# Queries and keys of pairs 1 to 7 laid out by transfers from a transposed input, in a fused attention and mixture kernel

## The chip, the cores and the metric

The kernel runs on one core of one Trainium2 chip. The metric is the device time of one execution in microseconds (us). TensorE is called PE below, its weight loads PEld; VectorE is DVE, ScalarE is ACT, GpSimd is POOL, and SP is the engine whose queue issues nearly all transfers.

## The reference, cut to what matters

Three stages follow each other. The change touches the first one alone, an attention in which a query sees only keys of its own cluster:

```
q_n, k_n, c_n = rows of q, k, centroids divided by (norm + 1e-6)
q_assign = argmax(q_n . c_n), k_assign = argmax(k_n . c_n)      # 16 clusters
mask   = q_assign == k_assign
scores = where(mask, 0.125 * q @ k.T, -1e9)
attn   = softmax(scores)
out    = attn @ v                                               # 2 batches, 8 heads, 768 x 64
```

The output, as 1536 tokens of 512 features, goes through a dense layer pair of width 2048 with softplus (`moe_w_in`, `moe_w_out`), and then through eight experts of width 1024 whose weights are mixed by a balanced gate (`moe2_*`). `moe_w_in` and `moe_w_out` arrive as float64 and are turned into float32 on the chip.

## The kernel before

Every product is taken with operands that are split in two: a rounded part (hi, type fp32r) and the remainder (lo), so that sums of products keep float32 accuracy.

The attention handles the 16 heads as 8 pairs `g` = 0 to 7, each of two heads `j` = 0, 1 of one batch. `w` = 0 stands for the query, `w` = 1 for the key. Per pair there is a preparation and then the attention itself.

The preparation of a pair: `pair_load` (L312) brings q, k and v as `raw` tiles, with the tokens on the partitions. `pair_split` (L326) makes hi and lo of q (scaled by 0.125) and k, side by side in `QS` and `KS`: for pair 0 on ACT and DVE, for the others on POOL (L344 to L346). `pair_trans` (L384) transposes them on PE, three blocks of 128 tokens into one PSUM tile `pt` (L393), eight such groups per pair; ACT copies each group to the tile `AT[w, j]` (L395), in which 64 rows hold hi and 64 rows lo; and a transfer copies the hi rows into `Bt[w, j]` (L397). `pair_norm` takes the squares of the raw tiles on ACT (L356), halves them three times on POOL and sums on DVE, and makes the norms. `pair_sims` (L401) multiplies the stacked `AT` by the normalised centroids in `Z` (L413), `pair_simsT` turns the result back, `pair_argmax` finds the cluster of each token, and `pair_ohT` transposes the one-hot codes into `OHT` and sends them by four transfers into rows 64 to 79 of the four `Bt` tiles (L476).

The attention of a pair has four halves of 384 queries each (head `j`, half `hf`), and each half six steps: `score` multiplies `AT` and then `Bt` (L532), where `Bt` adds the missing product of the two hi parts and the mask; DVE takes the maximum (L540), ACT the exponential (L545); `e_trans` transposes the result on PE (L572), ACT makes its hi part (L575) and DVE its lo part (L579); `av` multiplies by v (L587); `merge` finishes.

All groups that PE transposes or makes in the preparation, `pt` among them, and the transposed exponentials `t` share one PSUM pool of three tiles (`ps_t`, tag "t").

The order of the work is written as events with a step number; a pair takes `SP` = 24 steps, pair `g` begins its attention at step 24g, its scores 8 steps before. `sched_pair(g, b0)` places the preparation around `b0` = 24g - 34. The events are traced in the order of their steps, and a scheduler that works before the run then fixes the order of instructions on every engine, where it may bring an instruction forward. For the categories in `KEEP`, each instruction stays behind the last one traced so far on its engine.

`fetch_first` loads the float64 weights of the first unit of the dense layers (call 0, four transfers of 512 KB, L135 and L139) and converts them (calls 1 to 4) while the attention still runs; call 0 is placed at step 84 and is not in `KEEP`.

Of the kernel before, what the change touches and what calls it, by code (L numbers as in the profile page):

```python
# [7 lines left out]
F32 = mybir.dt.float32  # L8
# [11 lines left out]
@with_exitstack  # L20
def attention_moe_moe2(ctx, tc, q, k, v, centroids, w_in, w_out, w_gate, w1, w2, eye, out, dbg=None):
    nc = tc.nc
# [229 lines left out]

    Z = pp.tile([P, H, 224], F32R, tag="Z", name="Z", bufs=1)

# [7 lines left out]
    def prep_centroids():  # L262
        nc.vector.memset(Z.bitcast(F32), 0.0)
        craw = pp.tile([P, D], F32, tag="craw", name="craw", bufs=1)
# [18 lines left out]
    def prep_z(c2):  # L283
        for i in range(2):
            pc = ps_m.tile([P, P], F32R, tag="t", name=f"pc{i}")
            nc.tensor.transpose(pc, c2[:, i].rearrange("p a d -> p (a d)"), idr)
            nc.vector.tensor_copy(
                Z[:, :, 96 + 16 * i : 112 + 16 * i],
                pc.bitcast(F32).rearrange("p (h c) -> p h c", h=H),
            )  # L290

    def last_of_engines():
        found = {}
        for ins in reversed(nc.cur_bb.bb.instructions[-400:]):
            en = str(ins.engine).split(".")[-1]
            if en in ("PE", "DVE", "Activation", "Pool"):
                found.setdefault(en, ins)
        return found.values()  # L300
# [11 lines left out]
    def pair_load(g):  # L312
        b, hp = divmod(g, NPAIR)
        st = pairs[g] = Pair()
        st.b, st.hp, st.g = b, hp, g
        st.raw = []
# [7 lines left out]
        st.AT, st.Bt = {}, {}  # L324

    def pair_split(st, n):  # L326
        g = st.g
        rq, rk, rv = st.raw
        if n == 0:
            st.QS = pp.tile([P, 2, NT, 2 * D], F32R, tag="QS", name=f"QS{g}", bufs=1)  # L330
            st.KS = pp.tile([P, 2, NT, 2 * D], F32R, tag="KS", name=f"KS{g}", bufs=1)
        j, w = divmod(n, 2)
# [3 lines left out]
        else:  # L336
            hi, lo = st.KS[:, j, :, D:], st.KS[:, j, :, 0:D]
        if g == 0:
            sc = 0.125 if w == 0 else 1.0
            nc.scalar.activation(hi, r, AF.Copy, scale=sc)  # L340
            nc.vector.scalar_tensor_tensor(lo, r, sc, hi.bitcast(F32), ALU.mult, ALU.subtract)
            return
        if w == 0:
            nc.gpsimd.tensor_scalar(r, r, 0.125, 0.0, ALU.mult, ALU.add)  # L344
        copy_r(hi, r)
        nc.gpsimd.tensor_tensor(lo, r, hi.bitcast(F32), ALU.subtract)  # L346

    def pair_norm(st, n):
# [5 lines left out]
        if n < 2:  # L354
            r = st.raw[n]
            nc.scalar.activation(r, r, AF.Square, scale=8.0 if n == 0 and g else 1.0)  # L356
        elif n < 4:
# [43 lines left out]
    def pair_sims(st, hf, ph):  # L401
        g = st.g
        if ph == 0:
# [3 lines left out]
            st.sm = ps_m.tile([P, CB], F32, tag="t", name=f"sm{g}{hf}")  # L407
            n = 0
            for w in range(2):
                for j in range(2):  # L410
                    h = 2 * st.hp + j
                    o = 64 * w + 32 * j
                    nc.tensor.matmul(  # L413
                        st.sm, Z[:, h, 96 - o : 224 - o], st.AT[w, j][:, hf * CB : (hf + 1) * CB],
                        start=n == 0, stop=n == 3,
                    )
                    n += 1
        else:
# [61 lines left out]
    def sched_pair(g, b0):  # L480
# [8 lines left out]
        at(b0 - 12.13, lambda: pair_load(g))  # L489
        for n in range(4):  # L490
            P_(b0 - 7.54 + 1.5 * n, "sp", pair_split, n)
        for n in range(2):
            P_(b0 + n + 1.54, "sq", pair_norm, n)
# [3 lines left out]
        P_(b0 + (12.5 if g else 8.37), "nv", pair_norm, 6)  # L497
        for i in range(8):
            d = 1.09 * i
# [519 lines left out]
```

## Time and profile before

| | |
|---|---|
| median of 3 runs | 1630.16 us (1629.44 to 1633.29) |
| the profiled execution | 1626.59 us |
| its span, first to last instruction | 1624.8 us |
| mean granted PE clock | 0.995 |
| busy share of the span | PE 96%, PEld 86%, DVE 67%, ACT 53%, POOL 43% |
| last result of the attention begins (L603) | 300.9 us |

The span begins at the first instruction, so that all times of the trace are counted from there. Some 300 us of it are attention, the rest the two dense stages. Busy times are unions of the instructions' spans on one engine; since matmuls overlap in the pipeline, the time that a group of them costs is read from one group's start to the next one's start, not from the duration of one.

### The profile page before, as it was taken

The page shows a single profiled execution, that of the slowest core. Times are in us where ns is not written, and L with a number is a line of the kernel's source. Part 1 is how long each engine was busy: PE and PEld are TensorE (multiplying, and loading weights), DVE is VectorE, ACT ScalarE, POOL GpSimd, SP SyncE. Part 2 cuts the span into 40 slices and gives each one's busy share as a digit, 9 for nine tenths or more (in the row PEclk, how much of TensorE's full clock was granted, in tenths as well). Part 3 has the DMA queues.
Part 4 walks back from the last instruction along what each step waited for, and adds up shares of the span by engine and source line. Part 5 has one row for each costly group of instructions (what it writes and reads, how often), then busy time and mean ns, then how long its engine had stood idle before and what let it go on. Part 6 is the DMA issues. An engine that isn't in the chain of part 4 may idle for free.

```text
span 1624.8 us, 22972 instructions
## 1 busy us (share of the span) xinstructions
PE 1554.7 (96%) x8302; PEld 1392.2 (86%) x8302; DVE 1085.4 (67%) x1768; ACT 861.6 (53%) x1769; POOL 705.5 (43%) x729
## 2 busy tenths in 40 slices
PE   5999999889899989999999999999999999999999
PEld 5878888888797868899999999988999999999997
DVE  6998889998744677745556566577556556565553
ACT  6888888766666664434344344345434344343442
POOL 6544543233656652433344344345343443433330
PEclk9999999999999999999999999999999999999999
DMA  6233220256112121223222322314222232222311
GB/s 195 61 93 91 67 52 6 84 196 200 60 53 78 52 66 40 78 73 81 69 78 69 81 74 67 88 53 125 58 84 71 70 88 62 78 76 74 78 53 46
DMA packets 129474, 128.67 MB, mean 79 GB/s; under 512 B 8048, under 2 KB 99664, under 8 KB 129360
## 3 DMA queue, kind: packets, MB, share of 16 engines
q1 hardware_dynamic: 129216, 127.14, 27.7%
q8 instruction: 65, 1.06, 0.3%
q14 instruction: 49, 0.40, 0.1%
q10 hardware_dynamic: 144, 0.07, 0.0%
HBM read 107.72 MB, written 11.58 MB: 73 GB/s over the span
## 4 chain that ended last, share of the span: by engine, by line
PE 64%; DVE 6%; ACT 4%; issue 1%; POOL 1%; DMA 0%; DVEq 0%; SPq 0%; POOLq 0%; ACTq 0%
PE Y L813 32%; PE la L685 16%; PE mb L685 8%; PE lb L685 4%; PE y L794 2%; DVE gf L761 1%; DVE gl L775 1%; DVE wl L226 1%; ACT u L759 1%; ACT gh L774 1%; ACT u L758 1%; PE p L738 1%; ACT wh L225 1%; ACT u L760 0%; DVE xS L75 0%
## 5 line engine op out<-in xcount | busy, mean ns | idle before, releaser
L774 ACT CAST gh<-gf 128x384 fp32r<-128x384 f32 x316 | 161.3, 512 | 482.9 <-DVE gf L768 438.1
L214 POOL TENSOR_TENSOR wf<-wf 128x256 f32<-128x256 f32 x288 | 239.3, 852 | 351.7 <-DMA wf<-in_moe_w_dram 302.1
L232 POOL TENSOR_TENSOR w2l<-w2f,w2h 128x512 fp32r<-128x512 f32 x160 | 241.3, 1528 | 307.9 <-ACT w2h L231 307.9
L813 PE MATMUL Y<-w2h,gh 128*128 128x512 f32 x768 | 299.0, 389 | 0.6 <-ACT gh L774 0.6
L813 PE MATMUL Y<-w2l,gh 128*128 128x512 f32 x768 | 298.9, 389 | 0.0
L813 PE MATMUL Y<-w2h,gl 128*128 128x512 f32 x768 | 298.5, 389 | 0.0
L775 DVE TENSOR_TENSOR gl<-gf,gh 128x384 fp32r<-128x384 f32 x316 | 208.2, 662 | 96.0 <-ACT gh L774 89.3
L712 DVE TENSOR_TENSOR gf<-la,c 128x384 f32<-128x384 f32 x71 | 39.5, 557 | 253.3 <-PE la L685 253.2
L225 ACT CAST wh<-wf 128x512 fp32r<-128x512 f32 (+1 forms) x232 | 153.0, 684 | 35.1 <-PE la L685 24.3
L813 PEld LDWEIGHTS Y<-w2h,gl 128*128 128x128 f32 x768 | 144.2, 188 | 30.0
L813 PEld LDWEIGHTS Y<-w2h,gh 128*128 128x128 f32 x768 | 144.0, 187 | 22.2 <-ACT gh L774 1.1
L813 PEld LDWEIGHTS Y<-w2l,gh 128*128 128x128 f32 x768 | 144.2, 188 | 21.1
L768 DVE SCALAR_TENSOR_TENSOR gf<-gf,pb 128x384 f32<-128x384 f32 x177 | 153.6, 869 | 4.0
L226 DVE TENSOR_TENSOR wl<-wf,wh 128x512 fp32r<-128x512 f32 (+1 forms) x194 | 152.3, 811 | 1.5 <-ACT wh L225 1.5
L579 DVE TENSOR_TENSOR el<-t,eh 128x384 fp32r<-128x384 f32 x192 | 103.1, 547 | 18.9 <-ACT eh L575 17.4
L572 PE MATMUL t<-idf,E 128*128 128x128 f32 x576 | 97.9, 280 | 11.0 <-ACT OHT L471 3.7
L575 ACT CAST eh<-t 128x384 fp32r<-128x384 f32 x192 | 92.5, 484 | 24.1 <-PE t L572 12.5
L685 PE MATMUL mb<-chS,wh 128*128 128x384 f32 x288 | 98.2, 341 | 4.3 <-DVE gf L708 3.9
L231 ACT CAST w2h<-w2f 128x512 fp32r<-128x512 f32 x160 | 92.2, 617 | 16.8 <-PE y L794 8.6
L685 PE MATMUL la<-chA,wh 128*128 128x384 f32 x288 | 98.0, 340 | 1.7 <-DVE gf L768 1.7
L685 PE MATMUL la<-chS,wh 128*128 128x384 f32 x288 | 97.8, 340 | 0.3 <-ACT c L704 0.2
L540 DVE TENSOR_REDUCE sc<-s 128x1 f32<-128x768 f32 x96 | 90.8, 947 | 10.5 <-PE s L532 10.2
(210 smaller groups left out, 3524.6 us busy)
## 6 DMA issues: line engine op xcount, KB each, us to landing
w2f<-in_moe_w_dram SPq DMA_DIRECT2D x128, 256.0 KB, 3.3
wf<-in_moe_w_dram SPq DMA_DIRECT2D x128, 256.0 KB, 3.4
r<-in_moe_w_in_dram SPq DMA_DIRECT2D x16, 512.0 KB, 5.3
r<-in_moe_w_out_dram SPq DMA_DIRECT2D x16, 512.0 KB, 5.2
Bt<-AT SPq DMA_DIRECT2D x32, 192.0 KB, 2.7
pb<-pdram SPq DMA_DIRECT2D x15, 384.0 KB, 8.0
w<-wf SPq DMA_DIRECT2D x16, 256.0 KB, 3.7
w<-w2f SPq DMA_DIRECT2D x16, 256.0 KB, 3.4
```

Of the source, the lines that this page charges most:

```text
L214: nc.gpsimd.tensor_tensor(wf[:, SLOT[o_], :], wf[:, SLOT[u_], :], wf[:, SLOT[v_], :], ALU.subtract)
L225: nc.scalar.copy(wh[:, c0:c1], wf[:, c0 + o : c1 + o, :])
L226: (nc.vector if kind == 2 or u == (1, 0, 0, 0) else nc.gpsimd).tensor_tensor(wl[:, c0:c1], wf[:, c0 + o : c1 + o, :], wh[:, c0:c1].bitcast ...
L232: nc.gpsimd.tensor_tensor(w2l[:, c], w2f[c], w2h[:, c].bitcast(F32), ALU.subtract)
L572: nc.tensor.transpose(pt[:, t * P : (t + 1) * P], Et[i, t][:, s * P : (s + 1) * P], idf)
L575: nc.scalar.copy(eh, TT[i, s])
L579: nc.vector.tensor_tensor(el, TT.pop((i, s)), EHL[i, s].bitcast(F32), ALU.subtract)
L685: nc.tensor.matmul(ps, wt[:, s_, ks], xx[:, k_, :], start=i in (0, 1, 3) and n == 0, stop=n == 3 * nk - 1, skip_group_check=True,)
L768: nc.vector.scalar_tensor_tensor(g, src, 0.0, PB[sb, e][:, cols], ALU.max, ALU.mult)
L774: nc.scalar.copy(gh[:, cols], g)
L775: nc.vector.tensor_tensor(gl[:, cols], g, gh[:, cols].bitcast(F32), ALU.subtract)
L813: nc.tensor.matmul(y[m], gt[:, ms], wt[:, q, :], start=first and i == 0, stop=last and i == 2)
```

## The change

For pairs 1 to 7 the queries and keys are also given to the kernel transposed (`qt`, `kt`: 64 features by 768 tokens for each head, with the tokens in the order of the kernel's partition layout). The arrays are laid out on the host, ahead of the launch.

- `pair_load` brings two more tiles `rT` (128 partitions: two heads by 64 features; 768 tokens; 384 KB each) ahead of q, k and v.
- A new `pair_split_t` splits them in three phases: ACT writes hi of both heads at once (128x768, scaled for q); POOL scales the q tile and subtracts, 128x768 each; then for each head three transfers of 64 rows (192 KB each) put hi and lo into `AT` and hi into `Bt`: 12 transfers per pair in place of the four of L397. The third phase (`sp2`) is in `KEEP`, behind the last SP instruction alone.
- `pair_split` and `pair_trans` remain for pair 0. The raw q tile is no longer scaled in place, so the squares are taken with scale 1.
- `pair_sims` multiplies, for these pairs, the split tile `HL` of both heads by a `Z` that has one block per head: four matmuls per half as before. Pair 0 keeps the old form with a tile `Z0` of its own. `prep_centroids` clears `Z0` (128x448) on DVE and `Z` (128x768) on POOL, where DVE cleared 128x1792; `prep_z` fills both with six copies on DVE in place of two.
- `HL` takes the places of `QS` and `KS` (one buffer for each of q and k).
- `b0` is 24g - 38 for pairs 2 to 7, four steps earlier; pairs 0 and 1 keep theirs.
- `fetch_first(0)` moves from step 84 to step 14 and goes into `KEEP` (category `fr`, SP alone): its four loads come behind the last SP instruction traced by then.

```
+        if g:
+            for w, src in enumerate((qt, kt)):
+                t = pp.tile([P, S], F32, tag=f"rT{w}", name=f"rT{w}{g}", bufs=1)
+                nc.sync.dma_start(t, src[b, 2 * hp : 2 * hp + 2].rearrange("j d s -> (j d) s"))
+                st.rT.append(t)
...
+    def pair_split_t(st, w, ph):
+        g = st.g
+        r, sc = st.rT[w], 1.0 if w else 0.125
+        if ph == 0:
+            st.HL[w] = pp.tile([P, 2, S], F32R, tag=f"HL{w}", name=f"HL{w}{g}", bufs=1)
+            nc.scalar.activation(st.HL[w][:, 0], r, AF.Copy, scale=sc)
+            return
+        hi, lo = st.HL[w][:, 0], st.HL[w][:, 1]
+        if ph == 1:
+            if w == 0:
+                nc.gpsimd.tensor_scalar(r, r, sc, 0.0, ALU.mult, ALU.add)
+            nc.gpsimd.tensor_tensor(lo, r, hi.bitcast(F32), ALU.subtract)
+            return
+        for j in range(2):
+            js = slice(j * D, (j + 1) * D)
+            t = st.AT[w, j] = ap.tile([P, S], F32R, tag=f"AT{g % 2}{w}{j}", name=f"AT{g}{w}{j}", bufs=1)
+            u = st.Bt[w, j] = ap.tile([80, S], F32R, tag=f"Bt{g % 2}{w}{j}", name=f"Bt{g}{w}{j}", bufs=1)
+            for dst, src in ((t[w * D : (w + 1) * D], hi), (t[(1 - w) * D : (2 - w) * D], lo), (u[0:D], hi)):
+                nc.sync.dma_start(dst.bitcast(F32), src[js].bitcast(F32))
...
+                if g:
+                    c, m = Z[:, st.hp, 64 - 64 * w : 192 - 64 * w], st.HL[w][:, x]
+                else:
+                    o = 64 * w + 32 * x
+                    c, m = Z0[:, x, 96 - o : 224 - o], st.AT[w, x]
+                nc.tensor.matmul(st.sm, c, m[:, hf * CB : (hf + 1) * CB], start=n == 0, stop=n == 3)
...
-        for n in range(4):
+        for n in range(4) if g == 0 else ():
             P_(b0 - 7.54 + 1.5 * n, "sp", pair_split, n)
+        for w in range(2) if g else ():
+            for ph in range(2):
+                P_(b0 - 7 + 0.5 * ph + 3 * w, f"sp{ph}", pair_split_t, w, ph)
+            P_(g * SP - 31 + 2 * w, "sp2", pair_split_t, w, 2)
...
-        for i in range(8):
+        for i in range(8) if g == 0 else ():
             d = 1.09 * i
             P_(b0 + d + 0.5, "t0", pair_trans, i, 0)
...
-        sched_pair(g, g * SP - LEAD - 26)
+        sched_pair(g, g * SP - LEAD - (30 if g > 1 else 26))
...
-    at(92 - 8, lambda: fetch_first(0))
+    at(14, lambda: fetch_first(0), ("fr", 0))
...
-                for ins in last_of_engines():
+                for ins in last_of_engines(("SP",) if cat[0] in ("fr", "sp2") else ("PE", "DVE", "Activation", "Pool")):
```

## Rows read from the trace of the kernel before

**Rows 1.** The page: busy time of each engine over the whole span.
```profile
PE 1554.7 (96%) x8302; PEld 1392.2 (86%) x8302; DVE 1085.4 (67%) x1768; ACT 861.6 (53%) x1769; POOL 705.5 (43%) x729
```

**Rows 2.** Windows between the one-hot transfers: start:end, length, busy (instructions), clock, DMA share, GB/s.
```profile
core 0: us, PE busy (x) PEld busy (x) DVE busy (x) ACT busy (x) POOL busy (x), PEclk, DMA share, GB/s
50.83:89.40 38.57, 35.07 (x235) 31.14 (x233) 36.44 (x69) 33.81 (x78) 19.08 (x28) 1.00 0.24 64
89.40:124.84 35.44, 33.18 (x218) 28.46 (x218) 34.05 (x66) 31.19 (x73) 18.80 (x28) 1.00 0.38 107
124.84:159.14 34.30, 32.59 (x218) 28.46 (x218) 30.32 (x60) 29.80 (x71) 17.61 (x28) 1.00 0.37 102
193.27:227.40 34.13, 32.45 (x218) 28.51 (x218) 29.36 (x58) 29.69 (x71) 17.63 (x28) 1.00 0.21 53
261.54:295.67 34.13, 32.34 (x210) 29.15 (x210) 30.91 (x57) 28.30 (x63) 12.09 (x12) 1.00 0.04 7
```

**Rows 3.** Groups by line on PE, 193.27 to 227.40: count, busy us, mean ns.
```profile
L413 PE MATMUL sm<-AT,Z 128*128 128x384 f32 x8 | 1.8, 346 | 0.0
L393 PE MATMUL pt<-idr,KS 128*128 128x128 f32 x12 | 1.6, 245 | 0.0
L393 PE MATMUL pt<-idr,QS 128*128 128x128 f32 x12 | 1.6, 241 | 0.0
...
L427 PE MATMUL tp<-idf,sT 128*128 128x128 f32 x6 | 1.0, 272 | 0.0
L465 PE MATMUL po<-idr,OH 128*64 128x128 f32 x6 | 0.7, 224 | 0.0
```

**Rows 4.** Timeline of PE in that window: start, length, instruction, idle before.
```profile
198.77 0.45 PE L393 MATMUL pt<-idr,KS 128*128 128x128 f32 x3
199.29 0.55 PE L572 MATMUL t<-idf,E 128*128 128x128 f32 x3
...
200.67 0.38 PE L393 MATMUL pt<-idr,QS 128*128 128x128 f32 x3
200.88 0.52 PE L572 MATMUL t<-idf,E 128*128 128x128 f32 x3
...
204.23 0.34 PE L587 MATMUL av<-el,VV 128*128 128x384 f32 x1
204.89 0.55 PE L572 MATMUL t<-idf,E 128*128 128x128 f32 x3 [0.32 <-ACT AT L395]
```

**Rows 5.** Windows: the transposing part of that pair, then the rest of it.
```profile
193.27:206.60 13.33, 12.81 (x90) 11.22 (x90) 10.88 (x22) 13.11 (x33) 7.64 (x13) 1.00 0.47 116
206.60:227.40 20.80, 19.64 (x130) 17.29 (x129) 18.47 (x37) 16.57 (x40) 9.99 (x16) 1.00 0.05 12
```

**Rows 6.** Groups by line on ACT and POOL, 193.27 to 227.40.
```profile
L395 ACT CAST AT<-pt 128x384 fp32r<-128x384 f32 x8 | 3.8, 486 | 0.0
...
L356 ACT ACTIVATE rawq<-rawq 128x768 f32<-128x768 f32 x1 | 0.9, 862 | 0.0
...
L346 POOL TENSOR_TENSOR QS<-rawq,QS 128x384 fp32r<-128x384 f32 x2 | 2.0, 1017 | 0.0
...
L49 POOL TENSOR_SCALAR KS<-rawk 128x384 fp32r<-128x384 f32 x2 | 1.0, 514 | 0.1
```

**Rows 7.** Windows that hold one `Bt<-AT` copy, and two raw loads with one copy.
```profile
231.40:234.40 3.00, 2.93 (x19) 2.32 (x19) 2.46 (x4) 3.00 (x8) 2.77 (x5) 1.00 0.29 66
...
201.50:206.00 4.50, 4.18 (x32) 3.67 (x31) 3.95 (x8) 4.28 (x13) 2.81 (x6) 1.00 0.80 202
```

**Rows 8.** Timeline of SP's queue, one pair: start, time to issue, transfer.
```profile
193.27 2.44 SPq L476 DMA_DIRECT2D Bt<-OHT  x4
197.26 3.60 SPq L397 DMA_DIRECT2D Bt<-AT  x2
201.50 0.37 SPq L319 DMA_DIRECT2D rawq<-in_q_dram  x1
203.39 0.46 SPq L397 DMA_DIRECT2D Bt<-AT  x1
```

**Rows 9.** Start of the kernel: two windows with the granted clock, then the timeline.
```profile
20.00:24.00 4.00, 1.90 (x13) 1.41 (x13) 2.32 (x4) 1.66 (x4) 3.88 (x4) 0.54 0.55 147
24.00:28.00 4.00, 4.00 (x24) 3.83 (x23) 0.26 (x1) 2.80 (x7) 2.34 (x4) 0.61 0.46 95
...
9.51 0.47 DVE L287 CAST Z<-pc 128x128 fp32r<-128x128 f32 x2
...
22.57 0.50 PE L465 MATMUL po<-idr,OH 128*64 128x128 f32 x3 [0.48 <-DVE OH L458]
23.09 0.84 ACT L395 CAST AT<-pt 128x384 fp32r<-128x384 f32 x2
...
23.82 0.85 ACT L471 CAST OHT<-po 64x384 fp32r<-64x384 f32 x2
```

More of the change, by code (lines that the diff above doesn't have):

```diff
@@ L20, in attention_moe_moe2 @@
 @with_exitstack
-def attention_moe_moe2(ctx, tc, q, k, v, centroids, w_in, w_out, w_gate, w1, w2, eye, out, dbg=None):
+def attention_moe_moe2(ctx, tc, q, k, v, qt, kt, centroids, w_in, w_out, w_gate, w1, w2, eye, out, dbg=None):
     nc = tc.nc
@@ L251, in attention_moe_moe2 @@
         nc.gpsimd.memset(wsel[:, :, c : c + 1], float(NC_ - c))
-    Z = pp.tile([P, H, 224], F32R, tag="Z", name="Z", bufs=1)
+    Z = pp.tile([P, NPAIR, 192], F32R, tag="Z", name="Z", bufs=1)
+    Z0 = pp.tile([P, 2, 224], F32R, tag="Z0", name="Z0", bufs=1)
     def norm_newton(o, x, s0, eng):
@@ L262, in prep_centroids @@
     def prep_centroids():
-        nc.vector.memset(Z.bitcast(F32), 0.0)
+        nc.vector.memset(Z0.bitcast(F32), 0.0)
+        nc.gpsimd.memset(Z.bitcast(F32), 0.0)
         craw = pp.tile([P, D], F32, tag="craw", name="craw", bufs=1)
@@ L286, in prep_z, with last_of_engines @@
             nc.tensor.transpose(pc, c2[:, i].rearrange("p a d -> p (a d)"), idr)
[L287 to L294, printed above, removed]
+            pv = pc.bitcast(F32).rearrange("p (h j c) -> p h j c", j=2, c=NC_)
+            nc.vector.tensor_copy(Z0[:, :, 96 + 16 * i : 112 + 16 * i], pv[:, 0])
+            for j in range(2):
+                js, o = slice(j * D, (j + 1) * D), 64 + 32 * j + 16 * i
+                nc.vector.tensor_copy(Z[js, :, o : o + NC_], pv[js, :, j])
+    def last_of_engines(engines):
         found = {}
@@ L297, in last_of_engines @@
             en = str(ins.engine).split(".")[-1]
-            if en in ("PE", "DVE", "Activation", "Pool"):
+            if en in engines:
                 found.setdefault(en, ins)
@@ L315, in pair_load @@
         st.b, st.hp, st.g = b, hp, g
+        st.AT, st.Bt, st.rT, st.HL = {}, {}, [], {}
+        if g:
[3 more added lines that the diff above has]
+                st.rT.append(t)
         st.raw = []
@@ L323, in pair_load @@
             st.raw.append(t)
-        st.AT, st.Bt = {}, {}
     def pair_split(st, n):
@@ L329, in pair_split @@
         if n == 0:
-            st.QS = pp.tile([P, 2, NT, 2 * D], F32R, tag="QS", name=f"QS{g}", bufs=1)
-            st.KS = pp.tile([P, 2, NT, 2 * D], F32R, tag="KS", name=f"KS{g}", bufs=1)
+            st.QS, st.KS = (
+                pp.tile([P, 2, NT, 2 * D], F32R, tag=f"HL{w}", name=f"QK{w}", bufs=1) for w in range(2)
+            )
         j, w = divmod(n, 2)
@@ L337, in pair_split @@
             hi, lo = st.KS[:, j, :, D:], st.KS[:, j, :, 0:D]
[L338 to L341, printed above, removed]
-            return
[L343 to L346, printed above, removed]
+        sc = 0.125 if w == 0 else 1.0
+        nc.scalar.activation(hi, r, AF.Copy, scale=sc)
+        nc.vector.scalar_tensor_tensor(lo, r, sc, hi.bitcast(F32), ALU.mult, ALU.subtract)
+    def pair_split_t(st, w, ph):
[4 more added lines that the diff above has]
+            nc.scalar.activation(st.HL[w][:, 0], r, AF.Copy, scale=sc)
+            return
+        hi, lo = st.HL[w][:, 0], st.HL[w][:, 1]
[4 more added lines that the diff above has]
+            return
+        for j in range(2):
+            js = slice(j * D, (j + 1) * D)
[3 more added lines that the diff above has]
+                nc.sync.dma_start(dst.bitcast(F32), src[js].bitcast(F32))
     def pair_norm(st, n):
@@ L355, in pair_norm @@
             r = st.raw[n]
-            nc.scalar.activation(r, r, AF.Square, scale=8.0 if n == 0 and g else 1.0)
+            nc.scalar.activation(r, r, AF.Square, scale=1.0)
         elif n < 4:
@@ L407, in pair_sims @@
             st.sm = ps_m.tile([P, CB], F32, tag="t", name=f"sm{g}{hf}")
[L408 to L417, printed above, removed]
+            for n in range(4):
+                w, x = divmod(n, 2)
+                if g:
[4 more added lines that the diff above has]
+                nc.tensor.matmul(st.sm, c, m[:, hf * CB : (hf + 1) * CB], start=n == 0, stop=n == 3)
         else:
@@ L635, in attention_moe_moe2 @@
         at(175 + n * 5, lambda n=n: x_split("1_0", first_blk, n), ("xs", 0))
-    KEEP = {'sq': 1, 'red': 1, 'av': 1, 'am3': 1, 'tpa': 1, 'smc': 0, 'm0': 1, 'nw': 0, 'nv': 1, 'rw': 1, 'pz': 1, 'e1': 1, 'ln': 0}
+    KEEP = {'sp2': 1, 'fr': 0, 'sq': 1, 'red': 1, 'av': 1, 'am3': 1, 'tpa': 1, 'smc': 0, 'm0': 1, 'nw': 0, 'nv': 1, 'rw': 1, 'pz': 1, 'e1': 1, 'ln': 0}
     events.sort(key=lambda x: x[:2])
@@ L988, in attention_moe_moe2 @@
         run(steps.get(9, []))
-_INS = ["q", "k", "v", "centroids", "moe_w_in", "moe_w_out", "moe2_w_gate", "moe2_w1", "moe2_w2", "eye"]
+_INS = ["q", "k", "v", "qt", "kt", "centroids", "moe_w_in", "moe_w_out", "moe2_w_gate", "moe2_w1", "moe2_w2", "eye"]
 _OUTS = [((1536, 512), "float32")]
@@ L1004 @@
     inputs["eye"] = _np.eye(128, dtype=_np.float32)
+    for name in "qk":
+        a = _np.asarray(inputs[name])
+        b, h, n, d = a.shape
+        inputs[name + "t"] = a.reshape(b, h, 128, n // 128, d).transpose(0, 1, 4, 3, 2).reshape(b, h, d, n)
     for name in _INS:
```

## Prediction

> **What bounds the kernel now.** I read the page first: PE is busy for 96% of the span [rows 1], so a change pays when it takes time off PE's path. An average says nothing about one stage, so I cut the attention into windows that begin and end with the one-hot transfers of successive pairs [rows 2]. From 124.84 us on a pair takes 34.1 to 34.3 us, the same from pair to pair, and in each PE is busy for 32.5 us (95%), DVE for 29.4 to 30.3 (86 to 88%), ACT for 29.7 (87%). The two windows before that are longer, 38.57 and 35.44 us, and there DVE is the fullest engine, 36.44 and 34.05 us (94 and 96%): the weight conversions lie there. The window from 261.54 holds no preparation of a later pair, and shows what preparation costs: 210 matmuls in 34.13 us, where a pair with preparation has 218, of which 24 `pt`, 8 `sm`, 6 `tp` and 6 `po` [rows 2, 3] are preparation. The other 174 would take 34.13 x 174 / 210 = 28.3 us. Preparation thus costs 5.8 us per pair on the path that sets the end.
>
> Which part of the pair holds that cost? The part in which the eight `pt` groups are transposed, 13.33 us long, has PE busy for 12.81 and ACT for 13.11 us (98%) [rows 5]. In the rest ACT has 4.2 us free. So in the very stretch from which the change takes work, PE and ACT are both full, and DVE has 2.4 us to spare.
>
> **The change part by part, pairs 1 to 7.**
>
> PE loses the 24 `pt` matmuls. Their summed busy time is 3.2 us per pair [rows 3], but they overlap; from the start of one group of three to the next instruction it is 0.21 us [rows 4], so eight groups cost 1.7 us. Around them PE also waits for PSUM tiles that the copy of L395 has yet to free: 0.3 us of the 0.52 between the starts at 198.77 and 199.29, and 0.3 to 0.5 of the 0.66 between those at 204.23 and 204.89 [rows 4]. PE's gain per pair is therefore 1.7 us at least, 2.5 with these waits, and 3.2 if the full busy time counted. `sm` stays at eight matmuls of 384 columns, with other operands of the same shape: nothing.
>
> ACT loses eight copies of 486 ns, 3.8 us, and gains two of 128x768. No row shows this form; the square of the same shape takes 862 ns [rows 6], so 1.7 us. ACT gains 2.1 us per pair, and in the full stretch all 3.8, since hi is now placed at steps 3 and 6 of a pair, away from it.
>
> POOL loses 2 x 0.52 (L344, as L49), 4 x 0.51 and 4 x 1.02 us [rows 6], 7.2 in all, and gains one scaling and two subtractions of twice the size, 1.0 + 2 x 2.0 = 5.0 us. POOL is half idle [rows 2]; this gives nothing to the time.
>
> DVE has no term per pair. That is the limit of the gain: with 29.4 us of work at the 96% that it reached in the window of 89.40, a pair can't come under 30.6 us, a gain of 3.5.
>
> Transfers: one copy of 192 KB takes 0.29 of 3.00 us, 0.87 us of all 16 DMA engines, and a raw load (0.80 x 4.50 - 0.87) / 2 = 1.37 us [rows 7]. Eight more copies and two more loads are 9.7 us per pair, beside a share of 0.21 [rows 2] that is 7.2 us: 16.9 of about 31.5, so there is room on average. They are hidden by the lead: `sp2` stands at 24g - 31, the scores that read it at 24g - 8, 23 steps of 34.13 / 24 = 1.42 us, or 33 us. SP's queue takes on ten more instructions, some 0.4 us each [rows 8], 4 us of 34. What waits behind the `sp2` copies on SP are the loads of the next pair and then the one-hot transfers; without the cover, ACT would wait for `rT` (rival 3).
>
> The Trainium skill, "DMA: Bandwidth & Descriptors", section Rules for kernel authors, speaks against this step: two transfers to disjoint partition halves serialize, because both run on the same 16 engines. By that rule the twelve half-height copies cost twelve times one; the trace agrees as far as one copy already takes 0.29 of the engines' time over 3 us. The page's fabric ceiling of 435 GB/s (section Specifications) would make one copy 0.45 us, an estimate from that page, and twelve 5.4 us; by the row they are 10.4.
>
> The steps four earlier put the one-hot transfers (24g - 9 before, 24g - 13 after) further ahead of the scores. Issue and landing take over 2.44 us [rows 8], the old lead was about 1 step. PE filled that time with other work, so I count nothing, at most 0.5 us per pair.
>
> **Start.** Pair 1's 24 transposes lie at a time when PE is half idle and its clock at 0.54 and 0.61, so PE gains nothing there; the one-hot codes of pair 0 wait from 23.07 to 23.82 us behind two of pair 1's copies on ACT [rows 9], about 0.8 us that go. Four more `Z` copies of about 0.24 us on DVE [rows 9] cost at most 1 us; the smaller clear on DVE lies under the first load. Less PE activity could also leave the clock low for longer: the two windows of 4 us at half rate bound that at 2 us. I take -1 us, between -2 and +2.
>
> **Weights.** The first half of the float64 loads stood ahead of pair 1's raw loads and now goes behind; two `rT` loads of nearly the same size take its place. Nothing at the start. The conversions, which made the windows of 50.83 and 89.40 us long, run later; their work on DVE is the same, I take nothing.
>
> **Sum.** Four windows in which PE binds (124.84 to 261.54): 4 x 2.5 = 10. The two in which DVE binds: DVE is idle there for 2.1 and 1.4 us, I take 1 us each (0 to 2.5), 2 in all. Start 1. Together -13 us. A check from the other side: over these six windows, 211 us, PE has 198 us of work (32.5 taken for those not shown) and DVE 189; without `pt` PE has 188. Both engines at 95% would take 199 us, a gain of 12. What follows the attention starts that much earlier and is unchanged. The profiled execution took 1626.59 us with a span of 1624.8; it lies 3.6 us under the median of 1630.16, so I take the difference from the median: 1617. Bounds of the sum: 4 x 1.7 - 2 = 5 at the small end, 6 x 3.5 + 2 = 23 at the large one. About 0.3%, 5 us, is what a measurement of this kernel can tell from no change.
>
> **Rivals.**
>
> 1. Larger: PE's waits go too, and DVE at its limit sets the pair. 6 x 3.5 + 1 = 22 us, 1608. For it: DVE did reach 96%. Against: it does so where conversions fill gaps freely; in the normal pair it waits for ACT and PE.
>
> 2. Smaller: the `pt` groups were mere filling, and only ACT's 2.1 us per pair, of which half lies in free time, is won: 6 x 1 = 6, 1624. For it: PE, ACT and DVE wait for each other in a ring, so that one engine's relief is partly lost. Against: rows 5, ACT at 98% and PE at 96% in the same stretch.
>
> 3. Slower: ACT waits for `rT`. The loads of the next pair are placed about 5 steps behind the `sp2` copies, and hi 5 steps behind the loads, 14 us in all. Ahead of `rT` lie 12 x 0.87 = 10.4 us of copies, its own 1.4 and some 2 of latency: 13.8. There is no margin. If SP's queue starts the copies late, because they wait for POOL's lo or for the last score matmul that reads the old `AT`, ACT, which works in order, holds the exponentials behind hi, and PE follows. ACT has 4.4 us free per pair; from about 4.5 us late the gain of 2.5 is gone, at 6 us late each of six pairs loses 1 us net: 1636. Against: the loads don't depend on the copies, and the fixed order may put them ahead.
>
> 4. No net change, 1630: the start loses 2 us to the clock and the copies, and the extra waits on transfers eat half of each pair's gain.
>
> **Chances.** Forecast (8 to 18 us less) 0.52, rival 1 0.13, rival 2 0.13, rival 3 0.12, rival 4 0.10. Faster by over 0.3% are the forecast, rival 1 and most of rival 2: 0.75. Within 0.3%: rest of rival 2 and rival 4, 0.13. Slower: 0.12. The range from 1605 to 1628 holds forecast, rivals 1 and 2 nearly whole and the lower edge of rival 4; the likeliest case alone has 1612 to 1622.
>
> **What would show it.** The windows between one-hot transfers at 31 to 32 us for pairs 4 to 7, with PE about 30.5 busy and DVE over 92%; no `pt` row after the start; no waits of `t` for `AT`; attention ending 12 us or so before 300.9. Wrong would be: a wait of ACT at the hi split for `rT`, a PE wait at the first score of a pair for the copies into `AT`, windows still over 33 us, or a start longer by more than 2 us.

## The result: 0.8% less time, and the profile after

The changed kernel takes 1616.24 us (median of 4 runs, 1615.32 to 1620.68), the kernel before 1630.68 us beside it (4 runs). The ratio is 0.9918, 95% interval 0.9904 to 0.9932: 13 to 14 us less, where 13 were predicted. The profiled execution took 1615.32 us with a span of 1613.5, so its span is 11.3 us shorter than that of before.

The page's engine line, which answers to [rows 1]:

```profile
PE 1536.4 (95%) x8134; PEld 1381.5 (86%) x8134; DVE 1079.2 (67%) x1772; ACT 851.7 (53%) x1727; POOL 687.2 (43%) x681
```

PE has 168 matmuls less, seven pairs by 24. The windows between the one-hot transfers of the changed kernel, as in [rows 2]:

```profile
core 0: us, PE busy (x) PEld busy (x) DVE busy (x) ACT busy (x) POOL busy (x), PEclk, DMA share, GB/s
52.05:84.68 32.63, 29.03 (x180) 25.92 (x179) 29.87 (x59) 28.01 (x64) 15.78 (x21) 0.96 0.78 206
84.68:117.22 32.54, 29.89 (x195) 26.56 (x194) 30.40 (x61) 28.63 (x65) 15.86 (x21) 0.99 0.71 191
117.22:149.48 32.26, 29.69 (x196) 27.09 (x195) 30.77 (x62) 29.05 (x65) 16.22 (x21) 1.00 0.57 156
...
181.74:213.70 31.96, 29.72 (x196) 26.89 (x195) 29.22 (x59) 28.38 (x65) 15.35 (x21) 1.00 0.42 107
```

A normal pair takes 32.0 to 32.3 us instead of 34.1 to 34.3. In the last of these windows PE's busy time is 2.7 us below that of before, and the window 2.2 us shorter: half a microsecond of the relief comes back as waiting. The DMA share doubles there, from 0.21 to 0.42. The one-hot transfers were also moved, so the windows' edges are not the same point of the work. The attention's results are: they are written by DVE at L603 before and at L632 after, twice per pair. The starts, read from the timeline:

| first result of pair | 0 | 1 | 2 | 3 | 4 | 5 | 6 | last of all |
|---|---|---|---|---|---|---|---|---|
| before | 55.13 | 91.14 | 126.58 | 160.87 | 195.01 | 229.14 | 263.27 | 300.88 |
| after | 57.83 | 92.21 | 125.89 | 158.18 | 189.76 | 221.74 | 252.63 | 289.67 |
| after less before | +2.7 | +1.1 | -0.7 | -2.7 | -5.3 | -7.4 | -10.6 | -11.2 |

So the start loses 2.7 us, the two pairs with conversions win 1.6 and 1.8, the next four 2.0, 2.6, 2.2 and 3.2, and the end 0.6. What follows the attention keeps its length: -11.2 there, -11.3 in the span.

The groups by line of the changed kernel, 181.74 to 213.70, as in [rows 3] and [rows 6]; the last column is the idle time before them and what ended it:

```profile
L601 PE MATMUL t<-idf,E 128*128 128x128 f32 x72 | 12.0, 275 | 1.4 <-DVE el L608 0.8 <-ACT OHT L496 0.6
...
L366 POOL TENSOR_TENSOR HL<-rT,HL 128x768 fp32r<-128x768 f32 x2 | 3.7, 1848 | 1.4 <-ACT HL L360 1.4
...
L360 ACT ACTIVATE HL<-rT 128x768 fp32r<-128x768 f32 x2 | 1.7, 868 | 0.0
L442 PE MATMUL sm<-HL,Z 128*128 128x384 f32 x8 | 1.7, 337 | 0.0
...
L365 POOL TENSOR_SCALAR rT<-rT 128x768 f32<-128x768 f32 x1 | 0.8, 839 | 0.7 <-ACT HL L360 0.7
```

No `pt` is left, hi takes 868 ns (862 were assumed), the `sm` matmuls keep their duration, and ACT is nowhere idle for `rT` (0.0 before L360). The wait of the exponentials' transposes for the copy into `AT` [rows 4] is gone; those for DVE's lo part and for ACT's copy of the one-hot codes are there.

SP's queue for the pair with the copies from 184.28, as in [rows 8]:

```profile
169.35 0.34 SPq L325 DMA_DIRECT2D rT<-in_qt_dram  x1
173.36 0.33 SPq L325 DMA_DIRECT2D rT<-in_kt_dram  x1
...
181.74 2.44 SPq L501 DMA_DIRECT2D Bt<-OHT  x4
184.28 1.18 SPq L373 DMA_DIRECT2D AT<-HL  x2
185.56 0.55 SPq L373 DMA_DIRECT2D Bt<-HL  x1
...
193.02 0.59 SPq L373 DMA_DIRECT2D Bt<-HL  x1
193.72 0.54 SPq L330 DMA_DIRECT2D rawq<-in_q_dram  x1
```

The loads of the next `rT` go out as soon as POOL's lo has read the old one, 11 to 15 us ahead of the copies, not behind them; the hi that reads them starts at 196.91 us, 27 us after the load. The twelve copies fill the transfer engines from 184 to 194 us:

```profile
184.00:187.00 3.00, 3.00 (x22) 2.76 (x20) 2.28 (x5) 3.00 (x6) 2.08 (x4) 1.00 0.70 147
187.00:190.00 3.00, 2.42 (x15) 1.99 (x15) 2.86 (x6) 2.59 (x7) 1.85 (x3) 1.00 0.94 228
190.00:193.00 3.00, 3.00 (x21) 2.90 (x20) 3.00 (x10) 2.57 (x6) 0.00 (x0) 1.00 0.99 235
```

### The profile page after: what moved, and what is told of

It is laid out like the page before. It is cut to its first block, busy times and chain, and to the rows that moved or that the text cites. A ratio compares the mean times of both kernels' runs of the same rounds, so it can differ in the third digit from the quotient of the medians.

```text
span 1613.5 us, 22747 instructions
## 1 busy us (share of the span) xinstructions
PE 1536.4 (95%) x8134; PEld 1381.5 (86%) x8134; DVE 1079.2 (67%) x1772; ACT 851.7 (53%) x1727; POOL 687.2 (43%) x681
## 4 chain that ended last, share of the span: by engine, by line
PE 64%; DVE 7%; ACT 4%; issue 1%; POOL 1%; DMA 0%; DVEq 0%; ACTq 0%; POOLq 0%
PE Y L842 32%; PE la L714 16%; PE mb L714 8%; PE lb L714 4%; PE y L823 2%; DVE gf L790 1%; DVE gl L804 1%; DVE wl L226 1%; ACT gh L803 1%; ACT u L788 1%; ACT u L787 1%; PE p L767 1%; ACT u L789 1%; DVE xS L75 0%; ACT wh L225 0%
## 5 line engine op out<-in xcount | busy, mean ns | idle before, releaser
L608 DVE TENSOR_TENSOR el<-t,eh 128x384 fp32r<-128x384 f32 x192 | 101.5, 544 | 11.8 <-ACT eh L604 10.6
L733 ACT COPY c<-la 128x384 f32<-128x384 f32 x144 | 68.8, 478 | 57.2 <-PE la L714 55.9
```

The costliest lines, as they stand in the source:

```text
L608: nc.vector.tensor_tensor(el, TT.pop((i, s)), EHL[i, s].bitcast(F32), ALU.subtract)
```

## The experiments

Theory A is the prediction's: PE's relief is the gain, ACT's adds little, and the copies are hidden. Theory B is the rival that ACT's eight copies were the limit. Each kernel is the changed one with one edit, except f1 and f2, which are the kernel before with one part of the change. Every ratio is to the kernel before, timed beside it on the same chip (1628.5 to 1628.9 us); "to after" is the ratio less 0.9918, times 1630.7 us, and carries 2 us of the interval of the change itself. The last column is where the last result of the attention begins in the one profiled execution of each kernel. What follows it takes 1323.2 to 1328.0 us in these executions, though no edit touches it, so a difference between two last results is the cleaner reading of what an edit does to the attention. By it the edits cost 0.1 us (e10) to 45.5 us (e5), up to 5 us less than by the ratios.

| kernel | median us | ratio (95%) | to after, us | span, us | last result |
|---|---|---|---|---|---|
| after | 1616.24 | 0.9918 (0.9904 to 0.9932) | | 1613.5 | 289.67 |
| e1_pe_back | 1630.02 | 1.0008 (0.9999 to 1.0018) | +15 | 1626.5 | 302.70 |
| e2_act_back | 1623.15 | 0.9974 (0.9954 to 0.9995) | +9 | 1621.3 | 297.76 |
| e3_both_back | 1638.12 | 1.0060 (1.0039 to 1.0081) | +23 | 1639.7 | 312.58 |
| e4_lead26 | 1623.86 | 0.9970 (0.9959 to 0.9980) | +8 | 1620.9 | 295.54 |
| e5_copies_twice | 1663.68 | 1.0217 (1.0202 to 1.0233) | +49 | 1659.6 | 335.12 |
| e6_weights84 | 1624.39 | 0.9976 (0.9964 to 0.9988) | +9 | 1619.7 | 294.59 |
| e7_warm_start | 1619.57 | 0.9944 (0.9929 to 0.9959) | +4 | 1615.6 | 291.74 |
| e8_lo1_dve | 1619.82 | 0.9950 (0.9934 to 0.9967) | +5 | 1616.3 | 293.06 |
| f1_before_lead30 | 1635.54 | 1.0040 (1.0026 to 1.0053) | | 1633.7 | 305.67 |
| f2_before_weights14 | 1629.09 | 1.0000 (0.9988 to 1.0012) | | 1627.1 | 301.98 |
| e9_lead_by_pair | 1622.62 | 0.9958 (0.9942 to 0.9974) | +7 | 1620.0 | 294.96 |
| e10_lead26_to3 | 1618.13 | 0.9935 (0.9918 to 0.9952) | +3 | 1616.6 | 289.75 |

**PE's work given back (e1_pe_back).** Pairs 2 to 7 transpose 24 blocks again, into PSUM tiles that nothing reads.

```
+            for t in range(HT):
+                nc.tensor.transpose(st.pt[:, t * P : (t + 1) * P], st.HL[w][:, j, (hf * HT + t) * P : (hf * HT + t + 1) * P], idr)
...
+        for i in range(8) if g > 1 else ():
+            d = g * SP - 34 + 1.09 * i
+            P_(d + 0.5, "x0", pair_extra, i, 0)
```

> The changed kernel, with 24 more transposes per pair on PE for pairs 2 to 7, in eight groups of three at the steps of the old ones; their results are read by nobody, so no ACT copy comes back. Theory A (PE's path is what was won: 1.7 us per pair for the groups themselves, and some 0.8 us of waits for PSUM tiles that an ACT copy held): pairs 3 to 7 get 1.5 to 2 us longer, the whole 8 to 12 us, about 1626. Rival B (ACT's 2.1 us per pair was won, the transposes had been filling): pairs longer by less than 0.5 us, the whole by less than 3 us, about 1618. Rival C (what counts is the preparation moved four steps earlier): as B.

The gain is gone, +13 us in the span. The window between the first results of two successive pairs of this kernel (columns as above, here and below):

```profile
197.26:232.06 34.80, 32.35 (x220) 28.93 (x219) 29.44 (x59) 28.94 (x64) 15.26 (x21) 1.00 0.39 97
```

PE is back at 32.35 us with 24 matmuls more, ACT unchanged, and the pair is 2.8 us longer than its 31.98 in the changed kernel. Over the five pairs from the second on the loss is 0.7, 2.1, 4.7, 2.8 and 2.7 us; in the one of 4.7 the granted clock is 0.95 over 36.28 us, which explains 1.8 us of it at most. PE's share of the gain is thus all that A gave it, or a little more, as long as the rest of the change is in place. The unread groups also take turns in the three PSUM tiles of `ps_t`; this run doesn't separate that from PE's time.

**ACT's work given back (e2_act_back).** Eight copies of 128x384 per pair to a tile that nothing reads.

```
+            junk = pp.tile([P, CB], F32R, tag="junk", name=f"jk{st.g}{i}", bufs=1)
+            nc.scalar.copy(junk, st.HL[w][:, j, hf * CB : (hf + 1) * CB].bitcast(F32))
```

> The changed kernel, with eight more ACT copies of 128x384 per pair for pairs 2 to 7, at the steps of the old copies, from the split tile to a tile that nobody reads; no transposes come back on PE. Theory A (PE's path): ACT has some 4 us free per pair, so the 3.8 us of copies cost 0 to 1 us per pair, 0 to 6 us in all, 1616 to 1622. Rival B (ACT's path): at least 2 us per pair, 12 us or more, 1628 and above. Rival C (the steps): nothing, 1616.

```profile
161.02:194.85 33.83, 30.40 (x196) 26.93 (x195) 31.77 (x64) 31.74 (x74) 16.71 (x21) 1.00 0.64 177
```

With ACT at 31.74 of 33.83 us this pair is 2.2 us longer than its 31.6 in the changed kernel, and the span 7.8 us: between the theories, and some 60% of PE's price. The five pairs that hold the copies lose 0.7, 1.2, 1.3, 2.2 and 3.0 us, and not all of that is ACT's: the pair shown has 64 DVE operations where the changed kernel has 60 there, and in the one of 3.0 the granted clock is 0.95. B as the whole cause falls; A's "adds little" falls too.

**Both given back (e3_both_back).** The transposes of e1, and ACT's copies read them out of PSUM, as the old path did.

```
+            P_(d + 0.5, "x0", pair_extra, i, 0)
+            P_(d + 0.72, "x1", pair_extra, i, 1)
```

> The changed kernel, with both the 24 transposes and the eight ACT copies out of PSUM per pair for pairs 2 to 7, copied to a tile that nobody reads; the four steps, the transfers and the place of the weight loads stay as in the changed kernel. Theory A (PE, with the waits that the copies make): each pair back to about 34 us, 13 to 15 us more than the changed kernel, 1630. Rival C (the four steps earlier or the place of the weight loads carry part of the gain): clearly under that, for instance 1622 if half of it is theirs.

```profile
203.45:241.15 37.70, 34.57 (x220) 30.33 (x219) 30.30 (x58) 31.42 (x72) 15.18 (x21) 0.95 0.38 90
```

About 23 us over the change, nearly the sum of the two, and 9 us over the kernel before; 1.9 us of this pair at most is the clock, granted at 0.95. It would follow that what the change adds (hi on ACT, transfers, the order) costs some 9 us and the relief of both engines pays for it; but an order that was set for other work may cost by itself, and no run separates the two.

**The four steps undone (e4_lead26), alone (f1_before_lead30), and by pair (e9_lead_by_pair, e10_lead26_to3).**

```
# e4
-        sched_pair(g, g * SP - LEAD - (30 if g > 1 else 26))
+        sched_pair(g, g * SP - LEAD - 26)
# f1, on the kernel before
-        sched_pair(g, g * SP - LEAD - 26)
+        sched_pair(g, g * SP - LEAD - (30 if g > 1 else 26))
# e9
+        sched_pair(g, g * SP - LEAD - {0: 26, 1: 26, 2: 26, 3: 28}.get(g, 30))
# e10
+        sched_pair(g, g * SP - LEAD - (30 if g > 3 else 26))
```

> The changed kernel, with the preparation of pairs 2 to 7 at the old steps (b0 = 24g - 34), four steps later than in the changed kernel. Theory A, as predicted: the four steps are worth 0 to 0.5 us per pair, so 1616 to 1619. Rival C: the one-hot transfers come too late for the scores again, pairs longer by over 1 us, 1623 or more.

> The kernel before, with the preparation of pairs 2 to 7 four steps earlier (b0 = 24g - 38) and nothing else of the change. Theory A (the four steps pay only once PE and ACT are relieved, because the preparation then no longer binds there): within 3 us of before. Theory D (they are worth their 7 us by themselves, as undoing them cost): 1621 to 1623.

> The changed kernel, with the old steps (24g - 34) for pair 2, two steps earlier for pair 3 and the new ones (24g - 38) from pair 4 on. Theory (the four steps help from the fourth pair on, but crowd the start, where undoing them brought the first results 1.2 us and the third pair's 3 us sooner): 2 to 3 us less than the changed kernel, a ratio of about 0.990 to before. Rival (the order that the scheduler makes of it is no better): 0.992 or more.

> The changed kernel, with the old steps (24g - 34) for pairs 2 and 3 and the new ones from pair 4 on. Theory: as the run with steps by pair, 2 to 4 us less than the changed kernel, a ratio of 0.989 to 0.991 to before. Rival: the sudden step between pairs 3 and 4 costs what the start wins, 0.992 or more.

In e4 the first results come sooner (56.63, and 122.90 for pair 2 instead of 125.89), but from there a pair takes 33 to 36 us, and the kernel loses 8 by the ratio, 5.9 by the last result. The four pairs in which PE binds, from the first result of pair 2 to that of pair 6, take 136.69 us before, 126.74 in the changed kernel and in e4:

```profile
122.90:257.92 135.02, 124.10 (x778) 107.21 (x776) 123.27 (x239) 112.66 (x257) 59.05 (x81) 1.00 0.51 133
```

So with PE and ACT relieved but the preparation at its old steps, these pairs win 1.7 us in place of 10. PE does the same matmuls there (778, against 777 in the changed kernel) and is busy for 124.10 us instead of 118.53 at the same clock; why, no run shows. The groups by line of e4, 191.94 to 225.12, show a wait of PE that the changed kernel doesn't have there, the score matmuls waiting for ACT's exponentials:

```profile
L561 PE MATMUL s<-AT,AT 128*128 128x384 f32 x26 | 7.8, 362 | 1.3 <-ACT E L574 1.1
```

Put alone on the kernel before, the same four steps lose 6.5 us (f1; 4.8 by the last result, 2.8 of them ahead of the first result), with three pairs of 35.3 to 35.6 us where 34.1 to 34.3 stood. So they are neither free nor good in themselves: they are worth 6 to 8 us where PE and ACT have been relieved, and cost 5 to 6.5 where they haven't. I had expected 0 to 3 us from e4. e9 and e10 tried to keep the early start of e4 and the later pairs of the change. e10 leads by 2.7 us at pair 2 (123.20) and has given it all back by pair 4 (189.86, against 189.76); e9 loses its lead in two pairs of 36.1 and 37.2 us. Neither is faster than the change; which wait gives the lead back wasn't traced further.

**The copies twice (e5_copies_twice).** Each of the twelve copies per pair is followed by one of the same source to DRAM that nothing reads.

```
                 nc.sync.dma_start(dst.bitcast(F32), src[js].bitcast(F32))
+                dj = tc.dram_tile([D, S], F32, name=f"dj{g}{w}{j}{len(st.dj)}")
+                nc.sync.dma_start(dj, src[js].bitcast(F32))
```

> The changed kernel, with a second transfer of the same source rows to a place in DRAM behind each of the 12 copies of a pair: 24 instead of 12 transfers, the output is not touched. Theory A (the transfers are hidden by their lead of some 33 us): 0 to 3 us, 1616 to 1619. Rival 3 of the prediction (no margin: the transfers of the next pair's transposed rows come late and ACT waits in order): each pair 2 to 5 us longer, 1630 or more, with a wait of ACT at the hi split for the load.

```profile
189.67:227.94 38.27, 33.20 (x196) 27.68 (x195) 30.04 (x58) 29.31 (x65) 15.35 (x22) 0.96 0.78 196
```

The pair takes 38.3 us instead of 31.6, and no engine is full: PE is busy for 87% of it, the transfers for 78%. In the stretch of the copies the transfers are full, though, for more than twice as long as in the changed kernel:

```profile
191.00:194.00 3.00, 3.00 (x19) 2.41 (x18) 3.00 (x8) 2.72 (x8) 0.03 (x1) 1.00 1.00 235
194.00:200.00 6.00, 6.00 (x43) 5.50 (x43) 4.70 (x10) 5.15 (x13) 2.64 (x6) 1.00 0.95 223
200.00:206.00 6.00, 5.49 (x35) 4.68 (x35) 5.15 (x11) 5.24 (x13) 3.07 (x4) 1.00 0.97 219
206.00:212.00 6.00, 4.97 (x30) 3.96 (x28) 6.00 (x13) 2.73 (x6) 2.98 (x3) 1.00 0.98 260
```

The copies hold SP's queue from 185.96 to 206.7 us, 21 us instead of 9, and the second `rT` load goes out at 218.29, 3 us ahead of the next one-hot transfers instead of 8. The waits are spread over all engines, and none names `rT` or `AT`; which one sets the pair I could not tell. The whole loss lies in the attention, whose last result is 45 us later. Half of that falls on the first pair alone, 56.86 us where the changed kernel has 34.38:

```profile
55.03:111.89 56.86, 36.76 (x197) 30.39 (x198) 42.69 (x77) 34.04 (x72) 18.70 (x24) 0.82 0.69 192
```

There the float64 loads, issued from 52.72 us, stand in the same queue. So the cover of the copies is real and finite: twelve fit, twenty-four don't, and A's expectation for this run was wrong.

**The weights' place undone (e6_weights84) and alone (f2_before_weights14).**

```
# e6
-    at(14, lambda: fetch_first(0), ("fr", 0))
+    at(92 - 8, lambda: fetch_first(0))
# f2, on the kernel before
-    at(92 - 8, lambda: fetch_first(0))
+    at(14, lambda: fetch_first(0), ("fr", 0))
```

> The changed kernel, with the loads of the float64 weights back at step 84 and free to move forward, as in the kernel before. Theory A, as predicted: no difference, 1615 to 1618, with conversions in other places. Rival: the loads again stand in the start ahead of the second pair's transfers, or the conversions fall where DVE is full: 3 to 6 us more.

> The kernel before, with the float64 loads at step 14 behind the last SP instruction and nothing else of the change. Theory A (their place matters only beside the new transfers): within 3 us of before. Theory D (worth 7 us by itself, since conversions no longer crowd DVE in the first pairs): 1621 to 1623.

On the kernel before it is worth nothing (ratio 1.0000); undone in the changed kernel it costs 6 us of span, 4.9 by the last result, where I expected nothing. Two places show. One weight load goes out at 9.08 us, the next `rawv` (the third load of that name, so that of pair 2) slips from 20.32 to 24.71 us, right ahead of the one-hot transfers, and the first `Bt` score waits 3.09 us for these, against 0.89 in the changed kernel. The timeline of PE in e6:

```profile
30.75 1.11 PE L561 MATMUL s<-Bt,Bt 80*128 80x384 f32 x4 [3.09 <-DMA Bt<-OHT]
```

And the pair from 159.26 us has conversions that press on DVE, 33.42 us, and takes 35.39 instead of 31.6; the granted clock is 0.95 here, which explains 1.8 us of the 3.8 at most:

```profile
159.26:194.65 35.39, 31.34 (x196) 28.41 (x195) 33.42 (x64) 28.77 (x66) 15.69 (x21) 0.95 0.62 169
```

**The start (e7_warm_start, e8_lo1_dve).** e7 puts 36 unread transposes into the first 28 us, to keep PE at work; e8 has DVE make the lo part of pair 1, behind pair 0's one-hot codes, so that POOL's 128x768 subtraction doesn't lie beside DVE's small operations.

```
# e7
+        for i in range(8) if g == 1 else ():
+            P_(b0 + 1.09 * i + 0.5, "x0", pair_extra, i)
+        for i in range(4) if g == 0 else ():
+            P_(b0 + 19.77 + 0.001 * i, "x1", more_extra, i)
# e8
+        if ph == 1 and g == 1:
+            nc.vector.scalar_tensor_tensor(lo, r, sc, hi.bitcast(F32), ALU.mult, ALU.subtract)
+            return
```

> The changed kernel, with 36 transposes put into the start on PE whose results nobody reads: 24 of the split rows of pair 1, which stand where the kernel before had its real ones, and 12 of pair 0's similarity tile. Theory A (the start lost its 2.7 us because PE, idle from 15 to 24 us, ran at the lower clock level from 32 to 38 us): the granted clock is up earlier, the first results of the attention come 1 to 3 us sooner than in the changed kernel, 1613 to 1616. Rival (the start lost time to something else, as POOL and DVE slowing each other): no gain, or 1 to 2 us more for the transposes, 1616 to 1619.

> The changed kernel, with the lo parts of pair 1 alone made by DVE, in one operation each, behind pair 0's one-hot codes, in place of POOL in the middle of pair 0's argmax. Theory B of the start (POOL's 128x768 subtractions of 1.9 us made two DVE operations of pair 0's argmax take 1.46 and 1.23 us in place of 0.55 and 0.67): those two are short again, the one-hot transfers go 1 to 1.5 us sooner, 1614 to 1615. Theory A of the start (the clock): the argmax is shorter, but the low clock remains, and at most 1 us is won. If sims of pair 1, which now wait for DVE, are in the way: 1617 to 1619.

Both lose 2 to 5 us. In e7 pair 0's one-hot codes are ready 1.9 us later, the added transposes stand ahead of `po` in PE's order as well (27.27 us instead of 23.90), and the first `Bt` score starts at 31.56. The timeline of the changed kernel's start, as in [rows 9]:

```profile
16.00 3.89 POOL L366 TENSOR_TENSOR HL<-rT,HL 128x768 fp32r<-128x768 f32 x2
...
18.85 1.46 DVE L473 TENSOR_TENSOR A<-A,mx 128x384 f32<-128x384 f32 x1
...
19.86 2.62 POOL L388 TENSOR_TENSOR rawq<-rawq 128x384 f32<-128x384 f32 x3
...
20.34 1.23 DVE L475 TENSOR_TENSOR A<-A,wsel 128x384 f32<-128x384 f32 x1
...
23.90 0.85 PE L490 MATMUL po<-idr,OH 128*64 128x128 f32 x6 [7.94 <-DVE OH L483]
24.47 0.85 ACT L496 CAST OHT<-po 64x384 fp32r<-64x384 f32 x2 [6.46 <-PE po L490]
25.34 2.47 SPq L501 DMA_DIRECT2D Bt<-OHT  x4
28.29 0.95 PE L561 MATMUL s<-Bt,Bt 80*128 80x384 f32 x4 [0.89 <-DMA Bt<-OHT]
```

and that of e8:

```profile
18.83 0.65 DVE L476 TENSOR_TENSOR A<-A,mx 128x384 f32<-128x384 f32 x1
19.52 0.82 DVE L478 TENSOR_TENSOR A<-A,wsel 128x384 f32<-128x384 f32 x1
...
23.45 0.34 SPq L325 DMA_DIRECT2D rT<-in_qt_dram  x1
...
24.01 2.46 SPq L504 DMA_DIRECT2D Bt<-OHT  x4
...
29.41 1.62 PE L565 MATMUL s<-Bt,Bt 80*128 80x384 f32 x4 [3.11 <-DMA Bt<-OHT]
```

The expectation of e8 puts both slow DVE operations down to POOL's subtraction. By the rows that holds for the first (L473) alone; the second (L475) starts after the subtraction has ended, beside POOL's halving of `rawq` (L388), which before began at 22.26 us. e8 takes 1.2 us off the two and sends the one-hot codes 1.3 us sooner, but they land later, and PE waits 3.11 us for them: no net gain. As DVE now reads `rT` late, the load of the next one goes out at 23.45 instead of 17.84 us, right ahead of the one-hot transfers, as `rawv` did in e6. What both runs give is a second use of their traces. From the first `Bt` score to the third `av` matmul with the lo part, PE has the same matmuls in all kernels (47 to 51 of them are in the traces). That stretch in the kernel before, in the changed kernel, in f1 and in e7:

```profile
28.09:38.88 10.79, 8.04 (x51) 6.83 (x49) 8.52 (x17) 8.50 (x21) 5.62 (x11) 1.00 0.78 248
```

```profile
28.29:41.12 12.83, 10.98 (x50) 10.11 (x51) 8.76 (x17) 9.07 (x22) 1.59 (x5) 0.73 0.92 220
```

```profile
28.38:40.30 11.92, 10.07 (x50) 8.59 (x49) 8.68 (x17) 8.60 (x21) 6.36 (x12) 0.81 0.68 216
```

```profile
31.56:43.61 12.05, 9.87 (x51) 8.52 (x51) 8.77 (x17) 9.16 (x22) 1.59 (x5) 0.86 0.89 211
```

DVE and ACT do the same work in each; PE's busy time grows as the granted clock falls, and the stretch with it: 10.79 us at 1.00, 11.9 to 12.1 at 0.81 to 0.86, 12.83 at 0.73. But this stretch doesn't settle the start. f2, the kernel before with only the weights moved, has the low clock there as well, and its first result still comes at 55.10 us, where the kernel before has 55.13. Its stretch, and its way from there to the first result:

```profile
29.15:41.35 12.20, 10.46 (x47) 9.36 (x48) 9.25 (x17) 8.17 (x20) 7.66 (x13) 0.72 0.27 78
41.35:55.10 13.75, 12.98 (x91) 11.87 (x90) 13.44 (x26) 11.70 (x27) 1.84 (x3) 1.00 0.08 16
```

The same way in the kernel before and in the changed kernel:

```profile
38.88:55.13 16.25, 14.52 (x91) 13.16 (x90) 13.91 (x26) 12.13 (x28) 4.52 (x7) 0.89 0.07 13
```

```profile
41.12:57.83 16.71, 13.88 (x91) 12.14 (x91) 15.25 (x26) 14.31 (x32) 10.54 (x12) 1.00 0.31 89
```

The kernel before has its low clock here, at 0.89; at 1.00 the way takes 13.75 us in f2 and 16.71 in the changed kernel. There DVE is busy for 1.3 us longer than before with the same 26 operations, and one of them accounts for it: L582, 1.80 us beside POOL's subtraction (shown in the last section), which is L553 before:

```profile
41.09 0.50 DVE L553 TENSOR_SCALAR sc<-sc 128x6 f32<-128x6 f32 x1
```

## Why the prediction was right, and where its terms were off

**The mechanism held in part.** PE bound the normal pair, and the change took from PE. That this relief is needed e1 shows: PE's 24 matmuls given back cost the whole gain. That it is enough, as the prediction had it, e4 refutes: without the four steps the four windows in which PE binds win 1.7 us. By the table of first results they won 10.0 us in the changed kernel (10 predicted, 2.5 per pair, chosen between 1.7 and 3.2), and these 10 are the work of the relief and the steps together. It was put together wrongly in one point: I gave all of it to PE and none to ACT's relief outside its full stretch, but ACT's copies alone cost some 8 us when given back (e2, in part by clock and conversions). The two prices overlap: their sum is above the gain of these windows.

**The two windows with conversions** won 3.4 us, 2 predicted (0 to 5 as bounds). DVE's windows there fell from 94 and 96% busy to 92 and 93%.

**The start** was the term with the wrong sign: -1 predicted, between -2 and +2, and +2.7 measured. Up to the first `Bt` score it is +0.2: the wait behind pair 1's copies on ACT did go (from `po` to the copy of the codes 0.57 us, 1.25 before), but two DVE operations are 1.5 us longer beside POOL's subtraction and its halving, which the prediction didn't have. From there to the third lo `av` matmul it is +2.0, at a granted clock of 0.73 instead of 1.00. The prediction named this ("could also leave the clock low for longer", bounded at 2 us) and then counted none of it. From there to the first result it is +0.5, although the kernel before pays for its low clock in just this part. At 1.00 the way is 3.0 us longer in the changed kernel than in f2: DVE, the fullest engine there in both, spends 1.6 us more in the one operation beside POOL, and the four steps, which bring work of the next pair into it, lengthen it by 1.5 (16.71 against 15.25 in e4, where that operation takes 1.80 us as well). So the +2.7 can't be put down to the clock, and how it divides stays open. Why the clock falls is open too. In f1 PE is as busy as before between 20 and 28 us (6.29 and 5.90 us), and the clock still falls to 0.81; in f2, which leaves PE's operations as they were, it falls to 0.72; and e7's added work didn't restore it. Each kernel was profiled once, so that another execution may have its low stretches elsewhere.

**The four steps and the weights' place**, both taken as nothing, are each worth 5 to 9 us in the changed kernel by e4 and e6, and -6.5 and 0 on the kernel before. The prediction's reason for the first zero was that PE fills the time with other work; e4 doesn't bear that out. So the sum came within 1 us of the measured median with two zeros in it that were wrong, a start 3.7 us worse than forecast, and 2.0 us more won in the windows with conversions and at the end: the size of the whole was right partly by luck. The parts undone (e1, e2, e4, e6) add up to 32 us by the last results, nearly three times the gain, so none of them can be read as a share of it. That an order made for one placement loses by any single move would explain this, and each of the six other edits of the changed kernel loses or wins nothing; but it is argued, as no run sets the order anew for a part left out.

**Rival 3** (ACT waits for `rT` behind the copies) did not occur for the reason given against it: the loads depend only on POOL's lo, and they go out ahead of the copies. e5 shows that the copies become the limit at twice their number. **Rival 1** (DVE at its limit) did not occur: DVE is busy for 90 to 95% of a normal pair, and PE still waits for it 0.8 us. **Rival 2** (PE's groups as mere filling) is refuted by e1, but its ground, that one engine's relief is partly lost in the ring of PE, ACT and DVE, fits e4. What the prediction named as showing it: windows of 31 to 32 us came (31.96 to 32.26), PE at 29.7 instead of 30.5, DVE at 90 to 95% where over 92% was named; no `pt`, no wait of `t` for `AT`; the attention ended 11.2 us sooner where 12 were named. The start longer by more than 2 us was named as a sign of being wrong, and came.

**The transfers' price** was right: at a share of 0.99 they move 235 GB/s, so that a copy of 192 KB takes 0.84 us (0.87 used). By the Trainium skill, "DMA: Bandwidth & Descriptors", section Rules for kernel authors, two transfers to disjoint partition halves serialize; the trace agrees in that the twelve copies fill all engines for some ten microseconds, and one takes 4.0 us from issue to landing where it took 2.7.

## What to carry to other kernels

Look for the stretch inside a stage in which two engines are full at once, and price a relief by the pitch between groups on the path, not by busy time; but price the second engine too. A move of steps in a fixed order is no zero: its sign can depend on how full the engines around it are, so it is tried with the rest of the change and alone. Where a change takes early work from PE, read the granted clock of the stretch behind it, and where it moves POOL's work, read what DVE does beside it.

## What the runs showed of the hardware

- Some DVE operations are held up by whatever POOL runs when they start. In the argmax parts of the kernel before and of the changed kernel nine operations with two tensor inputs (128x384) start beside a POOL instruction, and each ends 0.40 to 0.42 us after that instruction does: L473 after 1.46 us, L475 after 1.23, where 0.54 to 0.55 is usual without POOL. The reductions (128x24 out of 128x384) take the same 0.53 to 0.55 us with POOL beside them and without. At pair 0's attention in the changed kernel a DVE operation on 128x6, 160 ns on the mean of the normal pair, lasts until POOL's subtraction ends (44.15 us):

```profile
41.98 2.17 POOL L366 TENSOR_TENSOR HL<-rT,HL 128x768 fp32r<-128x768 f32 x1
42.37 1.80 DVE L582 TENSOR_SCALAR sc<-sc 128x6 f32<-128x6 f32 x1
```

  The Trainium skill, "GPSIMD Engine Reference", section Specifications, says that POOL shares its memory interfaces with VectorE, and that DVE instructions with two tensor inputs, or in a mode that uses two ports, contend with it. The rows agree for L473 and L475, which read two tensors; in which mode L582 runs no run here shows.
- Where PE's clock is granted at 0.73, the same 50 matmuls keep PE busy for 10.98 us instead of 8.04, and the stretch, in which PE was busy for 75% before, is 2.0 us longer. In f2 such a stretch, 1.4 us longer at 0.72, leaves the first result where it was.
- Copies of 64 partitions within the chip's memory ran at 235 GB/s with all transfer engines at 0.99.
